# Delta-rule attention with a routed expert layer: the last four chunks with f made by VectorE, the turn and the sorting steps moved, and half-width masks

## The chip, the cores and the metric

One core of a Trainium2 chip. The metric is device time in microseconds (us) of one execution, as the median of several runs. TensorE is called PE, its weight loads PEld, VectorE DVE, ScalarE ACT, GpSimd POOL, and SyncE, which issues most transfers, SP.

## The reference

Two blocks follow each other. The first is a delta rule over 768 positions for 4 batches and 8 heads of 48 columns; its output, 3072 tokens of 384 values, goes into the second, a mixture of 4 groups of 4 experts.

```python
for t in range(S):
    kt, vt, bt = k_n[:, :, t], v[:, :, t], beta[:, :, t, None]
    y[:, :, t] = einsum('bhd,bhde->bhe', q[:, :, t], state)
    v_old = einsum('bhde,bhd->bhe', state, kt)
    state = state + bt[:, :, :, None] * einsum('bhd,bhe->bhde', kt, vt - v_old)
...
g_idx = argmax(x @ w_group)                # the token's group
e_idx = argmax(x[g_idx == g] @ w_expert[g])  # its expert in the group
h = maximum(x @ w1[g, e], 0.0)
out = softmax weights of g and e * (h @ w2[g, e])
```

k_n is k over its norm. A token goes to one expert of 16.

## The kernel before, in words

**Chunks.** The recurrence runs in 24 chunks (`NCH`) of 32 positions; the 128 partitions hold 4 batches of 32 positions. Within a chunk the dependence of the positions on each other is a triangular system; its inverse is made ahead, for four chunks at a time (`RG`), by many small VectorE steps (`inverse`, L273), and spread into `mtb` by ScalarE (L388). `gram` (L237) makes the products of keys with keys and queries ten chunks ahead (`LEAD`), so the last ten chunks have none of it beside them. `mask` (L264) cuts a chunk's query products to the causal part, twice side by side, each copy with the rows of every second batch set to zero (tile `gqm`, 512 columns). `scale` (L399) divides the values by the key norms (tile `vh`).

**One chunk** is `advance` (L410), a generator in four parts, resumed in turn by the loop over chunks (L768):

- the first puts `vh` into the PSUM tile `a_ps` by a product with the identity (L416), adds the keys' product with the state (L422), and copies it with its sign turned into `f` on ScalarE (L426); then it starts `o_ps` with the queries' product with the state (L431);
- the second multiplies `f` by the inverse (`w_ps`, L439); ScalarE copies it to `w` (L442);
- the third adds keys times `w` to the state, which stays in PSUM (`s_ps`, L449), and ScalarE copies the state in two halves to `s_bd` in SBUF (L455), where the next chunk's first two products need it;
- the fourth adds the masked query products times `w` to `o_ps` (L463, or four products by batch at L468 in the last ten chunks); ScalarE copies the result to `x` (L472), which SP stores to memory (L840).

**Routing** runs beside it, a chunk later. `logits` (L483) turns the 128 tokens of a chunk on PE (`t_ps`, L490), ScalarE copies them (`xt`, L496), and PE multiplies by the router's weights (`l_ps`, L500); ScalarE copies the result (`lg`, L502). `route` (L505) takes groups of chunks: 16 to 19 are one group, 20 and 21 the next, 22 and 23 the last. Its first half finds each token's expert (VectorE, L523 to L541); two products rank the tokens (`r_ps`, L547 and L548), ScalarE copies the ranks (`rk`, L553) and takes exponentials (`sx`, L554); its second half (L582 to L605, and `at`, L561) makes gates and one-hot places. A sorting step is two products (L621) that write token numbers by place into columns 384 to 479 of the state's first PSUM bank, beside the state, which has columns 0 to 383.

**Towards the first expert.** The places of the tokens of chunks 0 to 19 are copied out (`found`, L749), their rows gathered by GpSimd (L755) and turned into `x_ps` by products with the identity (`add_gathered`, L760). Chunks 20 to 23 (`near`) are still in SBUF: ScalarE multiplies their rows in place by whether they belong to the first expert (`only_first`, L742), and PE puts them to their places (`add_near`, L732; L729). Then come the sixteen experts (L964 and L983), with weights loaded two experts ahead.

**What sets the order.** Inside this stage each engine's order is written out by hand: the order of the calls is the order of each engine's queue. The tasks `inverse` and `route` are generators, too. A task either says what it waits for ("its turn", `SORT`, `PE_STEP`, `ACT_STEP` and so on), and `allow` (L676) then moves it one step at that place of the loop, or it says how much VectorE work it did, and `work` (L663) spends a budget on it, by shares. PSUM tiles with one buffer set an order as well: `a_ps`, `w_ps` and `r_ps` share one place ("s"), and `t_ps` and `l_ps` another ("g").

## Time and profile before

| what | us |
|---|---|
| median of 3 runs | 515.59 |
| lowest and highest | 514.5, 517.28 |
| the profiled execution's own time | 511.25 |
| its span | 509.0 |
| L422 of chunks 19, 20, 21, 22, 23 starts at | 192.02, 199.32, 206.44, 214.47, 223.39 |
| first product of the first expert (L964) starts at | 238.95 |

The profile shows one execution; its times count from the start of the span. A row of the timeline gives the start, the time from the first start to the last end of what it merges, engine, line, operation, tiles, shapes and how many instructions; in brackets stands the idle time of the engine before it and what ended that. Matmuls overlap, so consecutive rows of PE overlap by some 0.1 us and are compared by their starts. Each fp32 product is counted in two or more instructions: x32 of L422 is 16 calls. In the table by stage each engine has its busy time and, in brackets, its number of instructions; the last columns are the clock granted to PE, the share of the transfer engines and GB/s.

### The profile page before, as it was taken

What the parts mean: (1) busy time and instruction counts of PE and PEld (TensorE: products, weight loads), DVE (VectorE), ACT (ScalarE), POOL (GpSimd) and SP (SyncE); (2) the same over time, 40 slices, a digit from 0 to 9 for tenths busy, and PEclk for the clock granted to TensorE, in tenths of its full rate; (3) what the DMA queues carried; (4) which work ended last, traced back from release to release, by engine and by line L of the source; (5) the groups of instructions that cost most, each with busy time, mean ns of one, the idle gap of its engine ahead of it and who ended that gap; (6) DMA issues with size and microseconds to landing.
All of it is one profiled execution on the core that took longest, in us unless ns stands there. A gap on an engine that the chain in (4) does not pass through costs nothing.

```text
span 509.0 us, 18246 instructions
## 1 busy us (share of the span) xinstructions
PE 470.6 (92%) x7844; PEld 437.8 (86%) x7844; DVE 250.3 (49%) x829; ACT 188.9 (37%) x397; POOL 193.7 (38%) x288
## 2 busy tenths in 40 slices
PE   4346999999999999999999999999999999999993
PEld 3235878888888888889999999999999999999992
DVE  3999999999999995527312012102201121011110
ACT  3224768687676767652111111111111211111110
POOL 0040200633806425010445564466435654355231
PEclk9999999999999999999999999999999999999997
DMA  5781434444423546210798788769868978879740
GB/s 178 246 311 40 153 135 157 160 154 158 134 71 117 160 147 198 74 45 17 180 370 249 250 268 269 228 220 331 269 193 282 321 270 260 262 253 310 256 134 26
DMA packets 57333, 99.94 MB, mean 196 GB/s; under 512 B 18974, under 2 KB 41433, under 8 KB 57251
## 3 DMA queue, kind: packets, MB, share of 16 engines
q1 hardware_dynamic: 51331, 88.76, 52.7%
q0 software_dynamic: 5920, 10.00, 6.4%
q8 instruction: 63, 1.03, 0.8%
q14 instruction: 19, 0.16, 0.1%
HBM read 84.61 MB, written 14.27 MB: 194 GB/s over the span
## 4 chain that ended last, share of the span: by engine, by line
PE 57%; DMA 20%; DVE 7%; ACT 5%; SPq 4%; issue 4%; POOL 2%; DVEq 0%; POOLq 0%; ACTq 0%
PE y_ps L983 12%; PE h_ps L964 12%; DMA y_dram<-yq 9%; DMA out_dram<-yo,to_i 5%; PE w_ps L439 5%; PE s_ps L449 5%; DMA yr<-y_dram 5%; PE a_ps L422 3%; SPq L1023 3%; PE l_ps L500 3%; ACT s_bd L455 3%; PE o_ps L463 3%; PE o_ps L431 3%; PE g_ps L251 2%; PE a_ps L416 2%
## 5 line engine op out<-in xcount | busy, mean ns | idle before, releaser
L983 PE MATMUL y_ps<-hid,w 128*128 128x224 f32 (+15 forms) x768 | 132.2, 331 | 0.0
L983 PEld LDWEIGHTS y_ps<-hid,w 128*128 128x128 f32 x768 | 129.0, 190 | 0.3
L964 PE MATMUL h_ps<-xt,w 128*128 128x232 f32 (+14 forms) x720 | 122.7, 330 | 0.0
L964 PEld LDWEIGHTS h_ps<-xt,w 128*128 128x128 f32 x720 | 120.1, 190 | 0.3
L936 POOL DMA_INDIRECT xq<-x_dram,from_q x92 | 87.6, 952 | 36.5 <-issue 24.1
L986 DVE COPY yt<-y_ps 128x232 f32<-128x232 f32 (+13 forms) x14 | 5.1, 366 | 139.7 <-PE y_ps L983 139.7
L967 ACT ACTIVATE hid<-h_ps 128x448 f32<-128x448 f32 (+15 forms) x64 | 32.1, 502 | 100.2 <-PE h_ps L964 100.2
L995 POOL DMA_INDIRECT out_dram<-yo,to_i x32 | 34.1, 1066 | 91.5 <-DVE yo L1033 80.0
L988 ACT ACTIVATE yt<-y_ps 128x224 f32<-128x224 f32 (+15 forms) x34 | 11.5, 337 | 116.6 <-PE y_ps L983 116.6
L360 DVE TENSOR_TENSOR t<-m 128x81 f32<-128x81 f32 (+13 forms) x156 | 51.8, 332 | 0.2
L366 DVE TENSOR_TENSOR m<-m,t 128x81 f32<-128x81 f32 (+13 forms) x156 | 51.4, 330 | 0.0
L455 ACT ACTIVATE s_bd<-s_ps 48x768 f32<-48x768 f32 x46 | 37.0, 805 | 13.9 <-PE s_ps L449 13.3
L343 DVE SCALAR_TENSOR_TENSOR m<-m 128x29 f32<-128x29 f32 (+27 forms) x174 | 40.7, 237 | 0.4
L388 ACT ACTIVATE mtb<-mt,con 128x256 f32<-128x256 f32 x47 | 34.2, 741 | 1.6 <-DVE mt L377 1.5
L1033 DVE TENSOR_SCALAR yo<-yr,gate 128x384 f32<-128x384 f32 (+14 forms) x28 | 11.1, 416 | 43.0 <-DMA yr<-y_dram 35.4
L439 PE MATMUL w_ps<-f,mtb 64*64 64x48 f32 x768 | 28.0, 224 | 3.9 <-DVE mtb L386 3.9
L251 PE MATMUL g_ps<-kqt 48*32 48x64 f32 (+1 forms) x1216 | 18.5, 241 | 13.5 <-issue 8.8
L439 PEld LDWEIGHTS w_ps<-f,mtb 64*64 64x64 f32 x768 | 25.1, 138 | 6.2 <-ACT mtb L388 4.1
L422 PEld LDWEIGHTS a_ps<-s_bd,kqt 128*32 128x32 f32 x736 | 15.3, 111 | 15.5 <-ACT s_bd L455 7.3
L539 POOL TENSOR_TENSOR acc<-acc,hots 128x16 f32<-128x16 f32 x16 | 5.7, 354 | 60.1 <-DVE hots L537 59.1
L251 PEld LDWEIGHTS g_ps<-kqt 48*32 48x32 f32 x1216 | 14.6, 118 | 15.3 <-issue 10.5
L449 PE MATMUL s_ps<-w,kv 32*128 32x96 f32 x736 | 27.4, 286 | 0.1
(159 smaller groups left out, 603.5 us busy)
## 6 DMA issues: line engine op xcount, KB each, us to landing
w<-in_w_dram SPq DMA_DIRECT2D x29, 1536.0 KB
kv<-in_kv_dram SPq DMA_DIRECT2D x24, 448.0 KB, 4.1
kqt<-in_kq_dram SPq DMA_DIRECT2D x20, 512.0 KB, 4.2
x_dram<-x SPq DMA_DIRECT2D x24, 192.0 KB, 2.3
w<-in_w_dram SPq DMA_DIRECT2D x24, 128.0 KB, 3.7
y_dram<-yq SPq DMA_DIRECT2D x36, 84.0 KB, 9.2
yr<-y_dram SPq DMA_DIRECT2D x14, 192.0 KB, 2.5
kqt<-in_kq_dram SPq DMA_DIRECT2D x8, 256.0 KB, 3.5
```

The lines of the kernel that those rows point to most:

```text
L251: nc.tensor.matmul(g_out[quads[b], hh * NP + j, of], lhsT=kqt[rows, 0, j, quads[b]], rhs=kqt[rows, of, j, quads[b]], start=True, stop=True ...
L343: nc.vector.scalar_tensor_tensor(row, in0=m[:, j, 0:j], scalar=m[:, i, j:j + 1], in1=row, op0=ALU.mult, op1=ALU.add)
L360: nc.vector.tensor_tensor(tv, m[:, j + 2:, j:j + 1].to_broadcast([128, n, j]), m[:, j:j + 1, 0:j].to_broadcast([128, n, j]), op=ALU.mult)
L366: nc.vector.tensor_tensor(below, below, tv, op=ALU.add)
L388: nc.scalar.activation(mtb[:, rows, a], from_, ACT.Copy, scale=by)
L439: nc.tensor.matmul(w_ps[b, h], lhsT=mt[b, uu * H + (h % 2) * NP + h // 2], rhs=f[b, h], start=True, stop=True, skip_group_check=True)
L449: nc.tensor.matmul(s_at[:, b, j], lhsT=k[quads[b], j], rhs=w[quads[b], 2 * j:2 * j + 2], start=(u == 0 and j == 0), stop=True, skip_group_ ...
L455: nc.scalar.activation(s_bd[rows, :, :, hh, :], s_at[rows, :, :, hh * D:(hh + 1) * D], ACT.Copy)
L936: nc.gpsimd.indirect_dma_start(out=xq[:, g, :], out_offset=None, in_=x_dram[:, :].rearrange("n (q c) -> (n q) c", q=4), in_offset=bass.Ind ...
L964: nc.tensor.matmul(h_ps[:, k], lhsT=w1[:, j, (f + k) * 128:(f + k + 1) * 128], rhs=xt[:, j, 0:R], start=(j == 0), stop=(j == DC - 1), skip ...
L983: nc.tensor.matmul(y_ps, lhsT=w2[:, f, j * 128:(j + 1) * 128], rhs=hid[:, f], start=(f == 0), stop=(f == FC - 1))
L995: put = nc.gpsimd.indirect_dma_start(out=out[:, :], out_offset=bass.IndirectOffsetOnAxis(ap=to[0:P, i:i + 1], axis=0), in_=yo[0:P, :], in_ ...
```

## The change

- `mask` writes from chunk 14 on one causal copy of 256 columns in place of two of 512, and L468 reads it without the choice by batch; the constant `causal` (32 columns) is added to the first constant load. For all but chunk 1, the mask of chunk u+1 is queued at the head of chunk u instead of its end.
- In chunks 20 to 23 (`FREE` on) `a_ps` is begun by the first keys' product; the identity product L416 is gone. VectorE makes f = -a_ps - vh, reading `a_ps` from PSUM, in place of ScalarE's copy.
- In chunks 19 to 23 (`late`) the turn L490 goes behind w's product L439, ahead of the state update L449; the routing product L500 goes behind L468; the two ranking products go behind L449; and sorting steps go where the list `SORTS` has them: as many as its first number ahead of L449, its second behind L500.
- The group's task `route` is started at the next chunk, behind that chunk's f on VectorE.
- `only_first` of chunks 20 and 21 goes to the end of chunk 23. The first 128 gathered rows go into `x_ps` ahead of the count `n_ps` (L853), not at the head of the stage after chunk 23.

In the built program VectorE's queue has, from f of chunk 21: f, the first half of the group of chunks 16 to 19, its second half with its four `at`, `vh` and mask of chunk 23, f of chunk 22. Behind the last sorting, one reduction over 1440 columns (L887) stands after the copy of the experts' order (L645) instead of ahead of it.

```diff
+SHARE, SORTS = 0.64, [(0, 1), (0, 2), (0, 2), (2, 2), (0, 0)]
...
+        "causal": np.tile(i < k, (n_batch, 1)),
...
+        LATE, FREE = NCH - LEAD, NCH - RG
...
+            if u >= LATE:
+                gqs[u] = gqm.rearrange("p h a t -> p (h a t)")[:, 0:H * C].rearrange(
+                    "p (h t) -> p h t", t=C)
+                nc.vector.tensor_tensor(gqs[u], raws.pop(u), cut["causal"][:, None, :].to_broadcast(
+                    [128, H, C]), op=ALU.mult)
+                return
...
-            nc.tensor.matmul(a_ps.rearrange("p h d -> p (h d)"), lhsT=ident,
-                             rhs=vh.rearrange("p h d -> p (h d)"), start=True, stop=(u == 0),
-                             skip_group_check=True)
+            if u < FREE:
+                nc.tensor.matmul(a_ps.rearrange("p h d -> p (h d)"), lhsT=ident,
+                                 rhs=vh.rearrange("p h d -> p (h d)"), start=True, stop=(u == 0),
+                                 skip_group_check=True)
...
-                                         start=False, stop=True, skip_group_check=True)
+                                         start=(u >= FREE and j == 0), stop=True,
+                                         skip_group_check=True)
...
-            nc.scalar.activation(f, a_ps, ACT.Copy, scale=-1.0)
+            if u < FREE:
+                nc.scalar.activation(f, a_ps, ACT.Copy, scale=-1.0)
+            else:
+                nc.vector.scalar_tensor_tensor(f, in0=a_ps, scalar=-1.0, in1=vh, op0=ALU.mult,
+                                               op1=ALU.subtract)
...
-                        nc.tensor.matmul(o_ps[quads[b], h], lhsT=gq[quads[b], hq, b % 2],
+                        nc.tensor.matmul(o_ps[quads[b], h], lhsT=gq[quads[b], hq],
...
             for u in range(NCH + 1):
-                if u == NCH:
-                    add_gathered(gathered, [0])
                 step = advance(u) if u < NCH else iter([None] * 4)
                 turned = logits(u - 1) if u else iter([None] * 2)
+                if 0 < u < NCH - 1:
+                    mask(u + 1)
...
-                next(turned)
-                if u:
-                    allow(SPREAD)
+                late = FREE - 1 <= u < NCH
+                while late and waiting:
+                    start(*waiting.pop())
+                if not late:
+                    next(turned)
+                    if u:
+                        allow(SPREAD)
                 work(10)
-                if u < NCH:
+                if u < FREE - 1:
                     allow(SORT)
-                if u + 2 == NCH:
-                    allow(SORT)
-                if u == NCH - 1:
-                    for v in near[:2]:
-                        only_first(v)
...
                 next(step)
+                if late:
+                    next(turned)
+                    allow(SPREAD)
+                    for _ in range(SORTS[u - FREE + 1][0]):
+                        allow(SORT)
...
+                if not late:
                     next(turned)
-                else:
-                    next(turned)
-                allow(PE_STEP)
+                    allow(PE_STEP)
                 allow(ACT_STEP)
...
-                if NCH - 3 <= u < NCH:
-                    allow(SORT)
-                    if u + 2 == NCH:
-                        allow(SORT)
                 work(9)
                 if not ahead_of[u]:
                     next(step)
+                if late:
+                    allow(PE_STEP)
+                    allow(ACT_STEP)
                 next(step)
+                if late:
+                    next(turned)
+                    for _ in range(SORTS[u - FREE + 1][1]):
+                        allow(SORT)
+                if u == NCH - 1:
+                    for v in near[:2]:
+                        only_first(v)
...
-                    start(route(r), 0.6 if r == NGR - 2 else 1)
+                    if u < NCH:
+                        waiting.append((route(r), 1))
+                    else:
+                        start(route(r), 1)
...
-                if u + 1 < NCH:
-                    mask(u + 1)
+                if u == 0:
+                    mask(1)
...
             add_gathered(gathered, [1], [DC - 1])
+            add_gathered(gathered, [0])
```

More of the change, by code (lines that the diff above doesn't have):

```diff
@@ L17 @@
 RG = 4
-SHARE = 0.64
+SHARE, SORTS = 0.64, [(0, 1), (0, 2), (0, 2), (2, 2), (0, 0)]
 LEAD = 10
@@ L266, in mask @@
             like = [128, H, 2, C]
-            gqs[u] = wk.tile(like, F32, tag="gqm", name=f"gqm{u}", bufs=3)
+            gqm = wk.tile(like, F32, tag="gqm", name=f"gqm{u}", bufs=3)
+            if u >= LATE:
[4 more added lines that the diff above has]
+                return
+            gqs[u] = gqm
             nc.vector.tensor_tensor(
@@ L724, in deltanet_then_moe @@
             ahead_of = {u: [u + LEAD] if u + LEAD < NCH else [] for u in range(NCH + 1)}
-            begun, x_in = set(), {}
+            begun, x_in, waiting = set(), {}, []
             def add_rows(j, **how):
```

## The prediction

> **What bounds the kernel now.** I read the page first (share of the span and slices), then busy time by stage, then the PE timeline of one late chunk, then VectorE's and ScalarE's timelines beside it. A line number is that of the kernel before.

> ```profile
> span 509.0 us, 18246 instructions
> ...
> PE   4346999999999999999999999999999999999993
> ...
> DVE  3999999999999995527312012102201121011110
> ```

> PE is full from the fourth slice on, in both halves of the program. The stages that the change touches, cut at the first state product L422 of chunks 20 to 23 and at the first expert's L964:

> ```profile
> core 0: us, PE busy (x) PEld busy (x) DVE busy (x) ACT busy (x) POOL busy (x), PEclk, DMA share, GB/s
> 199.32:206.44 7.12, 6.96 (x208) 5.91 (x208) 2.33 (x12) 5.00 (x10) 1.81 (x3) 1.00 0.55 171
> 206.44:214.47 8.03, 7.87 (x216) 6.79 (x216) 3.85 (x15) 5.38 (x12) 0.00 (x0) 1.00 0.18 63
> 214.47:223.39 8.92, 8.77 (x223) 7.68 (x223) 3.01 (x12) 4.99 (x10) 0.00 (x0) 1.00 0.07 24
> 223.39:238.95 15.56, 15.04 (x240) 14.21 (x241) 7.81 (x38) 6.47 (x18) 2.15 (x2) 1.00 0.16 50
> 238.95:509.00 270.05, 261.44 (x1563) 260.16 (x1562) 47.31 (x96) 43.94 (x99) 125.89 (x141) 0.99 0.76 245
> ```

> PE idles 0.16 us in chunk 20 and hardly at all among the experts, so what the late chunks win, the span wins. But this PE is full because each wait has been filled. One chunk:

> ```profile
> 199.32 0.87 PE L422 MATMUL a_ps<-s_bd,kqt 128*32 128x96 f32 x32 [0.34 <-ACT s_bd L455]
> 200.00 0.84 PE L431 MATMUL o_ps<-s_bd,kqt 128*32 128x96 f32 x32
> 200.78 0.55 PE L490 MATMUL t_ps<-con,x 128*128 128x128 f32 x3
> 201.16 0.54 PE L621 MATMUL s_ps<-mine,at 128*128 128x48 f32 x4
> 201.63 1.14 PE L439 MATMUL w_ps<-f,mtb 64*64 64x48 f32 x32
> 202.70 0.84 PE L500 MATMUL l_ps<-wr,xt 128*128 128x20 f32 x6
> 203.47 1.15 PE L449 MATMUL s_ps<-w,kv 32*128 32x96 f32 x32
> 204.55 0.88 PE L468 MATMUL o_ps<-w,gqm 32*32 32x48 f32 x64
> 205.36 0.91 PE L416 MATMUL a_ps<-vh,con 128*128 128x384 f32 x2
> 206.44 0.87 PE L422 MATMUL a_ps<-s_bd,kqt 128*32 128x96 f32 x32 [0.16 <-ACT s_bd L455]
> ```

> The chain is state product, f, w, state update, copy of the state (s_bd, two ScalarE copies), next state product. The identity product L416 stands exactly where PE waits for that copy. VectorE in chunk 21, and one of its copies out of PSUM:

> ```profile
> 211.50 0.23 DVE L582 TENSOR_TENSOR rk<-rk,hots 128x64 f32<-128x64 f32 x1 [4.04 <-ACT rk L553]
> ...
> 214.08 0.69 DVE L268 TENSOR_TENSOR gqm<-gq,con 128x512 f32<-128x512 f32 x1
> 214.68 0.55 DVE L403 TENSOR_TENSOR vh<-kv,normt 128x384 f32<-128x384 f32 x1
> ...
> 252.48 0.56 DVE L930 COPY xt<-t_ps 128x384 f32<-128x384 f32 x1 [3.00 <-PE t_ps L928]
> ```

> A routing group's second half runs from 211.50 to 214.08 without a break; nobody waits for it at present.

> [...]the trace has 0.68 (L268) and 0.42 (L635). [...]f waits for all that is queued ahead of it. The trace agrees: w of chunk 23 starts at 226.84 although L439 ends at 226.47, because two copies (L742, 1.11 us) stand ahead.

> **The change part by part.** I rebuild the chunks from starts in the PE timeline: L422 to L431 0.69, L431 to what follows 0.77, L490 0.385, L439 1.065, L449 1.075, L468 0.815, L500 0.775, the two of L547/L548 0.50, a sorting step L621 0.47.

> *Masks and constant.* Ten masks fall from 0.68 to about 0.42 us, on VectorE ahead of PE (from 45 to 192 us PE waits 0.8 us for ScalarE and never for VectorE); a mask a chunk earlier delays an inverse by 0.6 us at most, and the last transposes L377 end at 164.7 and 195.0 for ScalarE steps at 167.25 and 196.37. Worth 0. If that cover failed, 0.6 us per group of four would show. The 32 columns more in the first constant load are 16 KB: 0.1 us at its 178 GB/s if it were awaited, 0 taken.

> *Identity product.* Four times 0.815 us leave PE, 3.3 us in all, but each lay under the state copy. The gain arises only if other work fills that place.

> *f by VectorE.* The trace has no such operation[...]. I take 0.56: L582 reads PSUM and SBUF in the last group and takes 0.19 us, no more than from SBUF alone. It starts 0.91 after L422 starts (0.87 and 0.04, as L930 after its transposes), and VectorE's hand-over to PE is 0.05 to 0.15 (ScalarE to L500 0.05; L561 to L729 0.15); 0.10 taken. So L439 starts 1.57 after L422, where L431 alone would let it at 1.46.

> *Turn behind w.* w's copy holds L449 until 1.72 after L439 starts (1.19, 0.49 and 0.04: 201.63, 202.82). The transposes L490 fit into it, 0.27 us stay empty. L500 goes under the state copy.

> *Sorting steps behind L500.* They write into the state's PSUM tile, beside its columns. In the program as built the first one after each state update waits for the second half of the state copy; in the old place that copy was long done. So they don't lie under it but behind it, 0.47 us each, on the chain: one in chunk 19, two in 20, 21 and 22. The state copy ends 2.97 after L449 starts (203.47 to 206.44).

> - Chunk 19: L422 192.02, L439 193.50, L449 195.22; ScalarE's queue (w, turn, two mtb of 1.27 together) puts the state copy at 196.74, done 198.43; a sorting step: chunk 20 starts at 198.90 (before 199.32).
> - Chunk 20: L439 200.47, L449 202.19, copy done 205.16 (L468 and L500 end earlier, 204.86), two steps: 206.10 (before 206.44).
> - Chunk 21: L439 207.67, L449 209.39, then L547/L548, L468, L500 until 212.56, copy done 212.36, two steps: 213.50 (before 214.47).
> - Chunk 22: ScalarE copies rk behind the state copy, at 212.32; VectorE starts 0.26 later, needs 2.58 up to the end of the group (211.50 to 214.08), 0.47 for vh and 0.33 for the mask, and only then comes f of chunk 22: 215.96, where it could have run at 214.41. L439 waits until 216.62, 1.55 us on the chain. Then L490 and two steps (from 217.69), L449 219.01, copy done 221.98, two steps: 222.92 (before 223.39).
> - Chunk 23: L439 224.49; L547 waits for w's PSUM: 226.21; L468 226.78, L500 227.60. The two copies L742, moved behind the last x, now stand ahead of the last turn's copy: L500's result at 228.49, L742 until 229.61, the last L500 0.54 later at 230.15 (before 230.64).
> - To the experts: the last routing steps keep their distance. The gathered rows' first tile (three products L729, 0.77 us) now lies behind them, ahead of the last near chunks. Before, these began at 234.82, of which 0.17 was a wait: 234.65 - 0.49 + 0.77 = 234.93, so 0.1 us later than before. The gather starts behind the last sorting step, at 222.9 (before 223.75), and stays hidden.

> Sum: +0.1 us. VectorE's new order gives the expert order some 1.6 us earlier (one reduction of 1.64 goes behind it), but the second expert's L964 did not wait for its weights. The profiled execution had 511.25 us around its span of 509.0; it becomes 511.35. It lies 4.3 below the median of the runs shown; the difference carried over to 515.59 gives 515.7.

> **Rivals.** About 0.5% (2.6 us) is what a measurement of this kernel can tell from no change.

> 1. *The sorting steps do fit under the state copy* (the wait ends with its first half). For: PE has 0.3 us to spare there in chunk 20. Against: the built program names the second half. Then chunks 20 to 22 win 0.4 to 0.5 us each: -1.2, 514.4.
> 2. *And f of chunk 22 does not wait.* For: the change queues a group's steps behind f, which is so for its first half. Against: the second half stands ahead of f. 1.55 more: -2.7, 512.9.
> 3. *f by VectorE is slow.* If an operand from PSUM and one from SBUF are read one after the other, f takes 1.2 instead of 0.56, all on the chain, four times: +2.6, and 518.3 in all with the 0.1. The place is between L422 and L439; f longer than 0.53 makes the change a loss already. Against: L582's 0.19.

> That the change doesn't do what it says: f of chunk 22 behind routing is that, and is in the sum.

> **How the numbers follow.** My sum, within 0.9 us, 0.61; the first rival 0.17; the second 0.14; the third 0.08. Four hand-overs of 0.05 either way, [...]and 1.55 to within 0.5 make the 0.9; the medians themselves spread by 2.8 us over three runs. Range 512.8 to 517.2: it reaches to the second rival and leaves out the third. Faster by over 0.5%: 0.15 (the second, and the first where the spread helps it); within 0.76; slower 0.09.

> **What would show it.** PE in chunk 22 idles some 1.5 us ahead of L439, released by VectorE; the sorting steps behind L500 show a wait for ScalarE's s_bd in chunks 19, 20 and 22; f takes 0.56; ScalarE's last turn copy stands behind L742; PE busy time from 192.02 to the experts falls by 3.3 while the stage stays 46.9 long. A stage under 45 us makes the second rival right, one over 49 the third.

## The result and the profile after

| | us |
|---|---|
| before, median of 20 runs | 516.86 (512.63 to 519.69) |
| after, median of 20 runs | 520.72 (514.80 to 523.14) |
| ratio after to before | 1.0055, 95% interval 1.003 to 1.0079 |
| after, profiled execution: own time, span | 523.08, 520.8 |

So the change makes the kernel slower by 0.55%, some 2.8 us (the medians above lie 3.9 apart), where no change was forecast. Ratios and their intervals, here and below, use the runs within 1.5% of a kernel's fastest, medians and clocks all runs; the profiled execution of after (523.08) lies just outside, so what it shows is looked for in other traces, too. Line numbers of after differ: the state product L422 is L432, w's product L439 is L454, the state update L449 is L464, L468 is L483, the turn L490 is L505, the routing product L500 is L515, the sorting step L621 is L636, the state copy L455 is L470, `only_first` L742 is L757, `at` L561 is L576, and the first expert's L964 is L992.

The page of after, its span, and its rows for PE and for the clock granted to it:

```profile
span 520.8 us, 18227 instructions
...
PE   4347999999999999889999999999999999999993
...
PEclk9999999999999998987999999999999999999998
```

PE is still nearly full, but the clock row has an 8 in slice 16 and an 8 and a 7 in slices 18 and 19. The table by stage of the same execution, cut at the state product of chunks 19 to 23 and at the first expert; behind the engines stands the granted clock (PEclk):

```profile
core 0: us, PE busy (x) PEld busy (x) DVE busy (x) ACT busy (x) POOL busy (x), PEclk, DMA share, GB/s
192.66:199.75 7.09, 6.37 (x205) 5.63 (x206) 3.74 (x9) 5.33 (x11) 5.61 (x11) 1.00 0.68 211
199.75:208.56 8.81, 8.38 (x210) 7.53 (x209) 1.45 (x3) 4.83 (x9) 0.28 (x1) 0.81 0.46 145
208.56:216.08 7.52, 7.31 (x214) 6.52 (x213) 3.62 (x18) 4.50 (x11) 0.00 (x0) 1.00 0.11 36
216.08:225.44 9.36, 7.66 (x219) 7.02 (x218) 2.92 (x11) 3.98 (x8) 0.00 (x0) 1.00 0.07 23
225.44:246.86 21.42, 20.14 (x242) 18.61 (x242) 9.92 (x49) 5.75 (x16) 2.18 (x2) 0.76 0.12 36
```

In before all five stages have 1.00. Its row for chunk 19:

```profile
192.02:199.32 7.30, 6.96 (x207) 5.90 (x208) 5.46 (x10) 4.93 (x10) 4.56 (x6) 1.00 0.57 180
```

In after chunk 20 has 0.81 and the last stage 0.76. The five take 54.20 us (before 46.93). The rest of this execution's 11.8 us is 0.64 ahead of chunk 19 and 3.9 among the experts (273.94 against 270.05). The 0.64 is within what the start of chunk 19 varies by (0.90 in the second trace below). The 3.9 is absent from that trace (270.12), and a part of it appears in an execution of before itself (271.54 in e8 below), at full clock; it does not come from the change alone, and its cause stays open.

That second trace (run e11_after_again) happened to keep its clock:

```profile
192.92:200.01 7.09, 6.37 (x205) 5.63 (x205) 3.02 (x7) 5.34 (x11) 5.62 (x10) 1.00 0.68 214
200.01:207.48 7.47, 6.96 (x210) 6.10 (x209) 1.45 (x3) 5.02 (x9) 0.00 (x0) 1.00 0.54 174
207.48:215.00 7.52, 7.31 (x214) 6.52 (x214) 3.62 (x18) 4.44 (x11) 0.00 (x0) 1.00 0.09 31
215.00:224.36 9.36, 7.66 (x219) 7.02 (x218) 2.92 (x11) 3.98 (x8) 0.00 (x0) 1.00 0.08 25
224.36:240.18 15.82, 14.99 (x242) 14.08 (x242) 9.92 (x49) 5.63 (x16) 2.18 (x2) 1.00 0.16 49
```

47.26 us for the same instructions, within 0.3 of before. So one program takes 47 or 54 us for this stage, by its clock. The difference of 6.94 is nearly all the clock: in the slower trace PE had half clock for 3.42 and for 10.24 us, 13.66 in all, and half of that is 6.83. What half clock does to one product: in that trace the queries' product L446 takes 1.53 us in chunk 20 (from 200.99, at half clock) and 0.84 in chunk 21 (from 209.25, at full clock).

Chunk 22 in this second trace shows what the forecast had as the new wait:

```profile
215.00 0.87 PE L432 MATMUL a_ps<-s_bd,kqt 128*32 128x96 f32 x32
215.68 0.84 PE L446 MATMUL o_ps<-s_bd,kqt 128*32 128x96 f32 x32
218.01 1.14 PE L454 MATMUL w_ps<-f,mtb 64*64 64x48 f32 x32 [1.48 <-DVE f L440]
219.07 0.55 PE L505 MATMUL t_ps<-con,x 128*128 128x128 f32 x3
...
222.27 0.84 PE L515 MATMUL l_ps<-wr,xt 128*128 128x20 f32 x6
223.34 1.09 PE L636 MATMUL s_ps<-mine,at 128*128 128x48 f32 x8 [0.22 <-ACT s_bd L470]
```

w's product waits 1.48 us for f, and the sorting steps wait for the state copy. VectorE has f behind the routing group's second half, as was forecast:

```profile
215.55 1.14 DVE L576 TENSOR_SCALAR at<-con,place 128x256 f32<-128x256 f32 x4
216.60 0.56 DVE L412 TENSOR_TENSOR vh<-kv,normt 128x384 f32<-128x384 f32 x1
217.06 0.42 DVE L273 TENSOR_TENSOR gqm<-gq,con 128x256 f32<-128x256 f32 x1
217.40 0.56 DVE L440 SCALAR_TENSOR_TENSOR f<-a_ps,vh 128x384 f32<-128x384 f32 x1
```

### The profile page after: what moved, and what is told of

Read it like the earlier page. It is cut to its first block, busy times and chain, and to the rows that moved or that the text cites. A ratio compares the mean times of both kernels' runs of the same rounds, so it can differ in the third digit from the quotient of the medians.

```text
span 520.8 us, 18227 instructions
## 1 busy us (share of the span) xinstructions
PE 476.3 (91%) x7836; PEld 442.6 (85%) x7836; DVE 249.8 (48%) x833; ACT 186.4 (36%) x393; POOL 193.1 (37%) x288
## 4 chain that ended last, share of the span: by engine, by line
PE 71%; DMA 8%; DVE 6%; ACT 5%; issue 5%; POOL 3%; another core or an unknown queue 1%; SPq 1%; POOLq 0%; ACTq 0%; DVEq 0%
PE h_ps L992 19%; PE y_ps L1011 18%; DMA out_dram<-yo,to_i 6%; PE w_ps L454 5%; PE s_ps L464 5%; PE a_ps L432 3%; ACT s_bd L470 3%; PE l_ps L515 3%; PE o_ps L446 3%; PE o_ps L478 3%; PE g_ps L253 2%; PE a_ps L426 2%; PE t_ps L505 2%; PE x_ps L744 2%; PE s_ps L636 1%
## 5 line engine op out<-in xcount | busy, mean ns | idle before, releaser
L992 PE MATMUL h_ps<-xt,w 128*128 128x232 f32 (+14 forms) x720 | 122.7, 330 | 0.0
L992 PEld LDWEIGHTS h_ps<-xt,w 128*128 128x128 f32 x720 | 120.1, 190 | 0.3
L964 POOL DMA_INDIRECT xq<-x_dram,from_q x92 | 87.6, 952 | 34.1 <-issue 25.3
L470 ACT ACTIVATE s_bd<-s_ps 48x768 f32<-48x768 f32 x46 | 37.0, 803 | 10.8 <-PE s_ps L464 10.3
L454 PE MATMUL w_ps<-f,mtb 64*64 64x48 f32 x768 | 29.0, 225 | 5.4 <-DVE mtb L395 3.0
L454 PEld LDWEIGHTS w_ps<-f,mtb 64*64 64x64 f32 x768 | 25.8, 140 | 8.8 <-ACT mtb L397 3.2
L464 PE MATMUL s_ps<-w,kv 32*128 32x96 f32 x736 | 27.3, 286 | 0.3
L432 PEld LDWEIGHTS a_ps<-s_bd,kqt 128*32 128x32 f32 x736 | 15.9, 114 | 12.4 <-ACT x L487 4.4
L464 PEld LDWEIGHTS s_ps<-w,kv 32*128 32x128 f32 x736 | 23.4, 192 | 2.7 <-ACT w L457 1.1
```

The source lines that it names most:

```text
L454: nc.tensor.matmul(w_ps[b, h], lhsT=mt[b, uu * H + (h % 2) * NP + h // 2], rhs=f[b, h], start=True, stop=True, skip_group_check=True)
L464: nc.tensor.matmul(s_at[:, b, j], lhsT=k[quads[b], j], rhs=w[quads[b], 2 * j:2 * j + 2], start=(u == 0 and j == 0), stop=True, skip_group_ ...
L470: nc.scalar.activation(s_bd[rows, :, :, hh, :], s_at[rows, :, :, hh * D:(hh + 1) * D], ACT.Copy)
L964: nc.gpsimd.indirect_dma_start(out=xq[:, g, :], out_offset=None, in_=x_dram[:, :].rearrange("n (q c) -> (n q) c", q=4), in_offset=bass.Ind ...
L992: nc.tensor.matmul(h_ps[:, k], lhsT=w1[:, j, (f + k) * 128:(f + k + 1) * 128], rhs=xt[:, j, 0:R], start=(j == 0), stop=(j == DC - 1), skip ...
```

## What halves the clock

The clock can be cut out stretch by stretch. In the profiled execution of after:

```profile
193.01:196.42 3.41, 3.30 (x115) 2.84 (x104) 3.31 (x8) 1.70 (x5) 1.99 (x7) 1.00 0.48 112
196.42:199.83 3.41, 2.81 (x102) 2.52 (x98) 0.12 (x1) 3.36 (x7) 3.41 (x4) 1.00 0.82 282
199.83:203.25 3.42, 3.42 (x80) 3.14 (x80) 1.45 (x3) 0.45 (x1) 0.20 (x1) 0.50 0.76 233
203.25:206.66 3.41, 3.29 (x124) 2.84 (x122) 0.00 (x0) 2.42 (x5) 0.00 (x0) 1.00 0.03 8
216.90:220.31 3.41, 1.93 (x69) 1.66 (x58) 2.13 (x7) 0.04 (x1) 0.00 (x0) 1.00 0.05 15
```

One long idle time did not halve it: the stretch from 216.90 has 1.48 us of idle in one piece, PE is busy for 1.93, and the clock afterwards is full. Ahead of 199.83 PE was busy for 2.81 of 3.41 us, its longest idle was 0.60, and still the clock fell.

What is different is what PE did. I count for every product the columns that it moves times the share of 128x128, the largest weights in these traces, that its own weights fill (array work): 128x384 with 128x128 weights gives 384, 48 columns on a 32x32 tile give 3. A product across the edge of a stretch counts by the share of its time. The identity product, two instructions of 384 in 0.815 us, would by that give some 3200 in 3.41 us (an estimate). The stretch from 196.42 to 199.83 holds the end of chunk 19: rest of the state update, four small products a head (L483, 64 of 32x32: 192), routing with 20 columns (L515: 120), sorting (L636, 48 columns: 192): 957 in all. The stretch with the long idle holds 1167. I laid this grid over all twelve traces that show a fall there, from 188 to 248 us (phase taken from the fall itself), and counted the stretches at full clock, apart by how long PE was busy in them:

| array work of a stretch | busy under 3.2 us: stretches, followed by half clock | busy 3.2 us and more: stretches, followed by half clock |
|---|---|---|
| under 1000 | 18, 13 | none |
| 1000 to 1300 | 12, 5 | 8, 0 |
| 1300 to 1500 | 4, 1 | 6, 0 |
| 1500 and more | 22, 0 | 106, 0 |

The limits (3.2 us, and the steps of work) are chosen to sort these stretches; they are no thresholds of the chip. All 19 falls come behind stretches that had both little array work and some idle time. Idle time alone did not do it: 22 stretches with idle time but 1500 or more of work kept the clock. Little work alone did not either, as far as it was seen: eight stretches of 1000 to 1300 kept the clock with PE busy throughout or nearly; none under 1000 was that busy. Five exceptions under 1000 remain (13 of 18), so the count goes with the falls, but alone does not decide them.

The same count outside this stage, from 53 to 188 us in all fourteen traces, agrees. Three of 517 stretches at full clock were followed by half clock (those from 72.45 in e5, 72.55 in e12 and 95.67 in e4, with work of 1226 to 1317 and 2.80 to 2.93 us busy), all among the eight that had under 1500 of work and under 3.2 us busy. So some of what lowers a mean clock lies ahead of the changed stage. (The counts in the expectations below are earlier estimates and differ from these.)

## The experiments

Three theories. *Array*: the change lowers the clock by what PE computes, because the identity products (128x128 weights, 384 columns, no time on the chain) left, and sparse products now follow each other. *Chain*: the clock is chance; what costs is f of chunk 22 behind routing, and sorting behind the state copy. *Idle*: PE's idle time lowers the clock.

Each run beside the kernel before on the same chip; the clock is the mean over a kernel's runs.

| run | median us | before | ratio [95%] | clock | before's clock |
|---|---|---|---|---|---|
| e1_dense | 518.78 | 516.99 | 1.0042 [1.0017, 1.0067] | 0.9903 | 0.9901 |
| e2_sparse | 524.10 | 516.99 | 1.0123 [1.0073, 1.0174] | 0.9850 | 0.9901 |
| e3_f_first | 516.87 | 516.99 | 0.9994 [0.9973, 1.0015] | 0.9859 | 0.9901 |
| e4_no_identity | 517.84 | 516.99 | 1.0002 [0.9974, 1.003] | 0.9890 | 0.9901 |
| e5_fill_two | 517.49 | 517.79 | 0.9986 [0.9961, 1.0011] | 0.9880 | 0.9891 |
| e6_fill_four | 520.11 | 517.79 | 1.005 [1.0026, 1.0073] | 0.9851 | 0.9891 |
| e7_before_fill | 516.84 | 517.79 | 0.9982 [0.9958, 1.0006] | 0.9926 | 0.9891 |
| e9_free_fill | 516.94 | 516.78 | 1.0004 [0.997, 1.0038] | 0.9890 | 0.9904 |
| e10_after_free_fill | 521.86 | 516.78 | 1.0056 [1.0025, 1.0088] | 0.9848 | 0.9904 |
| e11_after_again | 514.38 | 512.71 | 1.004 [1.002, 1.006] | 0.9890 | 0.9930 |
| e12_f_first_again | 513.54 | 512.71 | 1.0013 [0.9991, 1.0034] | 0.9885 | 0.9930 |

**e1_dense and e2_sparse.** To after, ahead of the routing product of chunks 19 to 22, products are added whose result nobody reads, into a second bank of the turn's tile: in e1 the identity product itself, in e2 32 products of 32x32.

```diff
+                if late and u < NCH - 1:
+                    nc.tensor.matmul(spare[u - 1].rearrange("p h d -> p (h d)"), lhsT=ident,
+                                     rhs=vhs[u + 1].rearrange("p h d -> p (h d)"), start=True, ...)
```

> The changed kernel with one addition: in chunks 19 to 22 the dense identity product (128 x 128 by 384 columns) stands where it stood before, ahead of the routing product, but writes into an unused PSUM bank and nobody reads it. Theory A (the clock): TensorE's granted clock fell to half for some windows because the four dense products are gone. Then the mean clock returns from about 0.984 to about 0.994, no half-clock stretch is left between chunk 19 and the first expert, and the time falls below the changed kernel's although 0.8 us of TensorE work is added four times: ratio to before 1.000 to 1.004. Theory B (the chain: f of chunk 22 behind routing, sorting steps behind the state copy, and the low clock is chance): 1.6 us more than the changed kernel, ratio 1.008 to 1.009. Theory C (idle time of TensorE lowers the clock): as A.

> As the run with the dense product, but the filler is 32 small products (32 x 32 by 48 columns), which take the same 0.8 us of TensorE and use a small part of its array; nobody reads them. Theory A (array work counts): the clock stays at about 0.982, ratio to before 1.007 to 1.011. Theory C (busy time counts): clock 0.994 and a ratio of 1.000 to 1.004, as with the dense filler. Theory B: ratio 1.008 to 1.009 in both.

The dense one brings the clock back to before's (0.9903 and 0.9901; 0.994 was expected), the sparse one (six runs) leaves it at after's 0.985. e1's own trace still has one halved stretch, behind 1407 among the near chunks. That speaks for array work. It does not exclude idle time, because e2's filler did not keep PE busy everywhere: in its trace it stalls in chunks 19 and 20, by 1.16 and 0.88 us:

```profile
198.87 0.36 PE L841 MATMUL t_ps<-vh,gqm 32*32 32x48 f32 x12 [1.16 <-issue]
```

Time is hardly won in e1: what the clock gives back, the dense product costs on the chain (1.0042, after 1.0055). e2 is 5.3 us slower than e1; by the mean clocks 2.7 of that is the clock.

**e3_f_first, and e12_f_first_again beside e11_after_again.** To after, the second half of the group of chunks 16 to 19 is held back until f of chunk 22 is in VectorE's queue. e11 is after itself, unchanged.

```diff
-SHARE, SORTS = 0.64, [(0, 1), (0, 2), (0, 2), (2, 2), (0, 0)]
+SHARE, SORTS = 0.64, [(0, 1), (0, 2), (0, 2), (0, 4), (0, 0)]
...
+            if r == NGR - 2:
+                yield BEHIND
...
+                allow(BEHIND)
```

> The changed kernel with the second half of the routing group of chunks 16 to 19 queued behind f of chunk 22 on VectorE, and that group's four sorting steps behind the state copy of chunk 22. The wait of 1.5 us ahead of w's product in chunk 22 goes; one sorting step more lies behind a copy (0.3 us). Theory B: 1.2 us less than the changed kernel, ratio to before about 1.003. Theory A: the same 1.2 us, but the clock stays at about 0.984 and half-clock stretches remain in the trace.

> The changed kernel once more, beside the next one. Array theory: its trace shows halved clock behind the stretch of chunk 19's or 20's end (850 to 1020 in 3.4 us) or of the last near chunks (390 to 980), two to four such stretches, clock 0.985, and at a clock of 0.9915 and more its runs lie less than 1 us above those of the kernel before. Chain theory: the whole difference to the kernel before stays at equal clock, 2.8 us. In chunk 22 the wait for f of 1.5 us again.

> The f-first kernel once more, on the same chip as the changed one. Chain theory: 0.8 us faster than it (chunk 22 takes 8.6 in place of 9.4), for the sorting steps that ran in the wait now stand behind the state copy. Array theory: 0.8 for the chain too, the clock as low as in the changed kernel (0.986), so slower than the kernel before at a lower clock, faster at the same.

Chunk 22 of e12:

```profile
217.96 0.87 PE L433 MATMUL a_ps<-s_bd,kqt 128*32 128x96 f32 x32
218.65 0.84 PE L447 MATMUL o_ps<-s_bd,kqt 128*32 128x96 f32 x32
219.51 1.13 PE L455 MATMUL w_ps<-f,mtb 64*64 64x48 f32 x32
...
224.19 1.99 PE L639 MATMUL s_ps<-mine,at 128*128 128x48 f32 x16 [0.22 <-ACT s_bd L471]
226.11 1.19 PE L433 MATMUL a_ps<-s_bd,kqt 128*32 128x96 f32 x24
```

The wait is gone, all four sorting steps now lie behind the copy, and the chunk takes 8.15 in place of 9.36. On the same chip the median falls by 0.84 (513.54 against 514.38). So the wait is real and worth about a microsecond. e3 did better than either theory had it: 0.9994, as fast as before at a clock lower by 0.004, where both had expected 1.003. By that, this order would be the faster one at equal clock; e12 (1.0013) does not repeat it.

The clock stays low in e11 and e12 (0.989, before 0.993). How much of after's loss on this chip is the clock can be told from the runs in three ways. By the mean clocks it is 2.1 of the 2.3 us between the means (worked out below). In runs whose clock was 0.9915 or more, after has a median of 513.15 (9 runs) and before 512.48 (33): 0.7 left of 1.7, and the 9 still have the lower mean clock (0.9931 and 0.9945). A straight line of time against clock through all 65 runs, with one slope, leaves 1.1 us of the 2.3 (give or take 0.7). So the clock is from half to nine tenths of the loss. The chain theory wanted none. Of the array theory's sizes the 0.985 did not come, and e11's trace has none of the two to four halved stretches that it expected.

**e4_no_identity.** To before, only this: chunks 20 to 23 lose the identity product, and VectorE makes f.

```diff
+            free = u >= NCH - RG
+            if not free:
                 nc.tensor.matmul(a_ps.rearrange("p h d -> p (h d)"), lhsT=ident, ...)
...
+            if free:
+                nc.vector.scalar_tensor_tensor(f, in0=a_ps, scalar=-1.0, in1=vh, op0=ALU.mult,
+                                               op1=ALU.subtract)
```

> The kernel before with one part of the change alone: in chunks 20 to 23 no identity product, f = -a - v by VectorE; order, masks and sorting as before. The product lay under the state copy, and f is covered by two groups of products behind it. Theory B: no change, ratio 0.999 to 1.001, clock as before. Theory A: TensorE has less dense work and the clock falls in some window between chunk 20 and the first expert: mean clock below 0.99, ratio 1.002 to 1.008, with nothing longer on the chain.

No change in time that the runs could tell, and the array theory's 1.002 to 1.008 did not come (1.0002); chunks 19 to 22 take 7.28, 7.11, 8.04 and 8.92 (before 7.30, 7.12, 8.03, 8.92), with 1.0 to 1.2 us of idle where the product was:

```profile
209.86 0.87 PE L424 MATMUL a_ps<-s_bd,kqt 128*32 128x96 f32 x32 [1.00 <-ACT s_bd L462]
```

The clock falls by 0.0011 only, against 0.004 in e11. So idle time in every chunk does little by itself, and the removal alone is not enough: with e1, which has the new order and a dense product, it takes the two together. The new order puts L483, L515 and the sorting steps in one row.

**e5_fill_two and e6_fill_four.** To e3, one dense product of 192 columns ahead of the routing product of chunks 19 and 22 (e5), and of chunk 23 and the one after it, too (e6).

```diff
+        def dense(u):
+            nc.tensor.matmul(spare[u], lhsT=ident, rhs=xlast[0][:, 0:DM // 2], start=True, ...)
...
+                    if u in (NCH - 5, NCH - 2):
+                        dense(u - 1)
                     next(turned)
```

> The f-first kernel plus one dense product (128x128 weights, 192 columns, result unused) ahead of the routing product of chunks 19 and 22. Counted as columns times the share of the array, the 3.4 us stretches whose successor fell to half clock there held 980 and 920[...]; one product adds 384. Array theory: no half clock in chunks 20 and 23, mean granted clock 0.986 -> 0.991, median 516.9 -> about 515.3, ratio 0.997. Chain theory (clock is chance): two more products of 0.45 us behind 0.2 to 0.3 of idle, 516.9 to 517.5, clock 0.986. Idle theory: 0.5 us of idle filled, clock up a little, no more than 0.988.

> As e5_fill_two, with the same dense product also ahead of the routing product of chunk 23 and of the one behind it, where the stretches hold 970 to 1080. Array theory: no half clock between chunk 19 and the experts, clock 0.993 to 0.995, median 514.8, ratio 0.996, the fastest so far. Chain theory: four products, one of them in an idle gap of 0.42: 517.5 to 518.5. Idle theory: like the chain theory.

e5 came halfway: clock 0.988 for the 0.991 expected. Its profiled run halved behind a stretch of chunk 20 (208.98 to 212.39, work 567), which had no product, and behind one of 1075 among the near chunks. e6 missed what both theories had: clock no higher than e3's (0.9851), 2.6 us slower than e5. Its run halved at 206.54, behind 721 in chunk 20, and again behind a stretch of 1229 among the near chunks. There the added product stands behind a wait for `xt` (0.42 us), and puts the routing product 0.65 us later. In chunk 20 both traces have a stall of PE inside L483, 1.01 and 1.28 us, within the very stretch that was followed by half clock. Such a stall takes work out of a stretch, leaves PE idle in it and costs its own time; it is a rival for a part of the loss that no run here sets apart.

**e7_before_fill and e8_before_again.** To before, the same dense product at two places: ahead of the routing product of chunk 23 and of the one after it. e8 is before itself.

```diff
+                if u >= NCH - 1:
+                    dense(u - 1)
```

> The kernel before with two of these dense products added in its sparsest stretch (ahead of the routing product of chunk 23 and of the one behind it), where it holds 860 to 1150 in 3.4 us. Array theory: added work makes it no slower: clock 0.990 -> 0.993, 516.3, ratio 0.9985. Chain and idle theories: 0.5 to 0.9 slower, 517.6, clock 0.990.

> The kernel before once more, for its trace. Array theory: if it shows half clock at all between chunk 16 and the experts, it is behind the stretch of 225 to 230 us (860 in 3.4 us) or that of 217 (1155), not within chunks 19 to 21. Chain and idle theories: no such place is marked out.

e7 came out as the array theory had it: two more products on the chain, and it is not slower; its clock is the highest of its chip, 0.9926 against 0.9891. (Its own trace still has one halved stretch, behind 916.) e8 shows where before loses:

```profile
223.49:226.90 3.41, 3.03 (x98) 2.60 (x98) 0.17 (x1) 1.27 (x4) 1.79 (x2) 1.00 0.26 76
226.90:230.31 3.41, 2.62 (x79) 2.29 (x78) 0.49 (x3) 2.27 (x7) 0.37 (x1) 1.00 0.29 88
230.31:233.73 3.42, 3.42 (x17) 3.34 (x17) 1.31 (x7) 0.98 (x2) 0.00 (x0) 0.50 0.18 62
233.73:237.14 3.41, 3.41 (x12) 3.15 (x13) 1.78 (x10) 1.10 (x3) 0.00 (x0) 0.50 0.00 0
```

The fall stands where the array theory put it, behind the sparsest stretch of this trace (work 512); its chunks 19 to 22 keep the full clock. So before is not free of this either: the trace that the forecast was worked from (clock 0.994) was one of its better executions. From 190 to 248 us, stretches at full clock with work under 1300 number 0 of 16 and 2 of 14 in the two traces of before, 3 of 12 and 4 of 16 in the two of after. With more such places, a grid that lies elsewhere in each execution should hit one more often; that is an estimate, and e11 had four and lost none.

**e9_free_fill and e10_after_free_fill.** To e3 and to after, one dense product of 128 columns behind each routing product from chunk 19 on, where PE waits for the state copy.

```diff
+            if u >= FREE - 2:
+                nc.tensor.matmul(both[:, 128:256], lhsT=ident, rhs=xt[:, 0], start=True, ...)
```

> The f-first kernel with one dense product of 128 columns (result unused) directly behind each routing product from chunk 19 on, where TensorE waits 0.2 to 0.3 us for the state copy anyway: 256 more of array work in each of the sparse stretches (525 to 1080 in 3.4 us) at nearly no time. Array theory: fewer halved stretches, clock 0.986 -> about 0.990, median 516.9 -> 515.5, ratio 0.997. Chain theory: 516.9 to 517.3 (products of 0.3 us, hidden in all chunks but the last two), clock 0.986. If the stretches inside runs of products for which the profile names no releaser move with the instructions' positions, chunk 20 or 23 shows one of 0.2 to 1.3 us at another place than before.

> The changed kernel with the same products and nothing else. Array theory: clock 0.985 -> about 0.989, median 520.7 -> 519.0, ratio 1.0055 -> 1.002. Chain theory: no gain, 520.7 to 521.2, clock 0.985.

e9 raised the clock as expected (0.986 to 0.989, though on another chip) and won no time. e10 did neither: clock 0.9848 and 521.86 us, as the chain theory had it, though it is after plus dense work. In both a stall appears in chunk 20, inside a run of products, with no releaser named:

```profile
203.85 0.61 PE L484 MATMUL o_ps<-w,gqm 32*32 32x48 f32 x36
205.22 0.53 PE L484 MATMUL o_ps<-w,gqm 32*32 32x48 f32 x28 [0.76 <-issue]
```

This is e9; e10 has 0.86 there, and its stretch with that stall held 889 and was followed by half clock.

## Why the forecast was wrong

- *f by VectorE*: right. 0.547 to 0.559 us in every trace that has it, for the 0.56 taken; L930 of before, a copy of 384 columns out of PSUM, takes 0.56, too. ScalarE's copy that it replaces takes 0.49 (L426), so f itself is no faster. The third rival is out; its 1.2 was an estimate for two passes.
- *Chunk 22*: right. f late by 1.48 for 1.55.
- *Sorting steps behind the state copy*: right in chunks 20 and 22, with 0.22 to 0.32 us of waiting ahead of them, released by `s_bd`. In chunk 19 the wait is 0.61, and the profile of after and of e11 puts its end to `at`, made by GpSimd, which the forecast left out; it fits that chunk's 0.21 us over the forecast. The first rival is out. The second needed a change of the program (e3) and is worth 0.8 to 1.2 us then.
- *The periods*: right within 0.3 us as long as the clock is full. Forecast 6.88, 7.20, 7.40, 9.42 and 16.1 us (the last to the experts); 7.09, 7.47, 7.52, 9.36 and 15.82 in e11, of which 0.38 in chunk 20 is a stall inside L483. Stage 47.26 for "stays 46.9 long".
- *Masks*: taken as 0 and not tried alone. In traces with no half clock ahead of it, chunk 19 starts between 191.96 and 192.92 in seven with the new masks (193.83 in e10), and between 192.02 and 192.51 in three with the old. A cost of a few tenths can't be told from that.
- *PE busy time*: fell by 2.3 in e11 (45.59 to 43.29), not by 3.3. The number of sorting products is the same over the stage, so they are not the reason; it stays open. No effect on the end.
- *The sign for the third rival*: "one over 49" came (54.20) and misled, for f took its 0.56; the forecast had no sign for the clock.
- **The step that failed**: "Four times 0.815 us leave PE, 3.3 us in all, but each lay under the state copy. The gain arises only if other work fills that place." The removal was costed at nothing, and the sum carried all PE durations over from an execution at full clock, and the 4.3 us from that execution to the median with them, as if halved stretches came as often in both kernels. The product had no place on the chain, but it was the densest work of its stretch. With it gone and the sparse products in a row, the mean clock fell by 0.004 (e11: 0.9930 to 0.9890). By estimate, a halved stretch of 3.41 us lowers the mean over 513 us by 0.0033 and costs 1.7 us (after's profiled execution lost 6.94 in 13.66 us of half clock), so 0.004 are 1.2 stretches more an execution, or 2.1 us of the 2.3 between the means (515.18 and 512.91). The line through all runs gives the clock less, about half; what is left beside it, 0.2 to 1.1 us, is not traced to a part of the change. No rival and neither end of the range had a term for the clock, though the stage table has a column for it.

That the clock is the larger part of the loss is shown: one program takes 47 or 54 us for the stage by its clock, the mean clock of e11 is 0.004 below that of before beside it, and the first runs of after have 0.9851, below before's on every chip (0.9891 to 0.9930). That the missing dense work lowers it is supported by e1, e4, e7 and the table of stretches, but not by every run: e6 and e10 added dense work and the clock did not rise, each with a stall in chunk 20. In these traces little work and some idle time came together ahead of every fall; which of the two the clock follows, and how, was not shown. A version clearly faster than before was not found: e7 and e5 have the lowest ratios, and both intervals reach over 1.

## What to carry to other kernels

A product that hides under a wait can still earn its place (the mean clock was 0.9851 in after, 0.9903 in e1 with the dense products back): before it is removed, add up the array work of the 3.4 us around it, the stretch of these traces, and look where small tiles and few columns would then follow each other with gaps between them. Read the granted clock by stage in more than one execution of the old kernel, since one trace may be a lucky one (here 0.994, where before's means are 0.9891 to 0.9930). And where the clock differs between executions, compare two kernels at equal clock first: that parts the chain from the clock.

## What was not expected of the hardware

- PE busy for 2.81 of 3.41 us and halved afterwards, and busy for 1.93 of 3.41 and not halved. No fall came behind a stretch with PE busy for 3.2 us or more (120 stretches in the table), and none behind one with 1500 or more of array work (128).
- Added work that costs no time: e7, 0.9982 with two more products (interval 0.9958 to 1.0006).
- Stalls of 0.38 to 1.28 us inside a run of PE products, with no releaser named, in chunk 20 of e1, e5, e6, e9, e10, e11 and e12 (36 or 38 product instructions into L483), and of 1.16 and 0.88 us in the fillers of e2 (chunks 19 and 20). None is in chunk 20 of the first trace of after, of e3, or of the traces with the old order (before, e4, e7, e8). Shorter ones, 0.18 to 0.40 us, stand inside w's product of chunk 23 in all traces but before, e11 and e12, the old order too. What PE waits for there was not tried and stays open.
